# Gated linear attention with a mixture of adapters: a hand-written order of work on all engines, suffix decay, and loads by chunk

## The chip, the cores and the metric

One core of one Trainium2 chip. A core has five engines with an instruction queue each: PE (TensorE, matmuls and transposes), DVE (VectorE), ACT (ScalarE), POOL (GpSimd) and SP (SyncE, which here only issues DMAs). Each runs its queue in order and waits on semaphores for the others. The metric is device time in microseconds of one execution.

## The reference

Four batches, 8 heads, 768 positions, head dimension 48. First a linear attention whose state decays by a gate, then a mixture of 8 adapters of rank 16, of which the best two by a gate count:

```python
for t in range(S):
    state = alpha[:, :, t, :, None] * state + np.einsum('bhd,bhe->bhde', k[:, :, t], v[:, :, t])
    y[:, :, t] = np.einsum('bhd,bhde->bhe', q[:, :, t], state)
...
logits = x @ w_gate                      # x: y with the 8 heads side by side, 3072 x 384
...                                      # softmax over the two largest of 8
delta[mask] += w[mask, k, None] * (x[mask] @ A[e] @ B[e])
return x + delta
```

## The kernel before, in words

A batch has 6 chunks of 128 positions, so there are 24 units (batch, chunk), done in order, since the state passes from chunk to chunk. All 16 input loads (four batches of alpha, k, q, v, 1.18 MB each), the weights and the 24 stores go through SP's queue; batch 3 is issued when the second batch's work begins.

`prologue` (L129) serves two chunks at once. ACT takes the logarithm of alpha (L133); PE sums it along the chunk with a triangular matrix of ones (`cum`, L139) and in total per head pair (L141); ACT makes exp(-cum), exp(cum) and exp(total) (`ainv`, `acum`, `dec`, L145 to L149). POOL multiplies k by `ainv` into `kg` (L151), q by `acum` into `qg` (L153) and casts v into `vb` (L156).

`unit` (L159) does one chunk. PE transposes `kg` and `qg` (`tr`, L165, eight transposes), DVE copies them out (`kq`, L169). PE makes the new state `kv`: an identity matmul brings in the old one (`sbd`, L174), four matmuls add k times v (L179); DVE multiplies by `dec` into the other `sbd` (L186). PE makes the attention scores `at` (L194), DVE masks them (`at_sb`, L198). PE sums `y` from the old state (L206) and from the scores (L214).

Then the mixture: ACT copies `y` out (`xb`, L220), PE transposes it (`xt`, L223), DVE copies that (`xs`, L225), PE makes `z`, the 128 adapter values and 8 gate logits (L228). The gate is a chain on DVE with one stop on ACT: `mx` (L231), `df` (L233), `ex` on ACT (L235), `wu` and its sum `den` (L238), `rd` (L242), `zw` (L244). PE transposes `zw` (`zt`, L248), DVE copies it (`zs`, L250), PE adds the delta into `y` (L251), ACT copies `y` into `o` (L253), SP stores it (L255).

The order of the instructions on each engine is not the order of this text: the framework's scheduler chose it when the program was built, by priority and by its own estimate of when inputs are ready. Once chosen it is fixed. PSUM has one buffer for `cum`, one for `tr`, one for `at` (two banks), two for `y`, and two shared by `kv`, `xt`, `z` and `zt` (tag `m`).

Of the kernel before, what the change touches and what calls it, by code (L numbers as in the profile page):

```python
# [41 lines left out]
def kernel(  # L42
# [86 lines left out]
    def prologue(b, g, ring):  # L129
        a_t, k_t, q_t, v_t = batches[b]  # L130
        cs = slice(g * G, (g + 1) * G)
        lg, qg, kg = lgs[ring], qgs[ring], kgs[ring]
        nc.scalar.activation(lg[:, :, :, 0:D], a_t[:, cs], AF.Ln)  # L133
        acum = scal.tile([P, G, H, D], F4, name="acum")
        ainv = scal.tile([P, G, H, D], F4, name="ainv")
        dec = scal.tile([P, G, NP], F4, name="dec")
        for c in range(G):
            cum = ps_cum.tile([P, 512], F4, name="cum")
            nc.tensor.matmul(cum[:, 0:DM], tri[:, :], lg[:, c, :, 0:D], start=True, stop=True)  # L139
            for p in range(NP):  # L140
                nc.tensor.matmul(  # L141
                    cum[:, DM + p:DM + p + 1],
                    lg[:, c, 2 * p:2 * p + 2, :].rearrange("a b s -> a (b s)"), ones[:, :],
                    start=True, stop=True)
            nc.scalar.activation(  # L145
                ainv[:, c].rearrange("p h d -> p (h d)"), cum[:, 0:DM], AF.Exp, scale=-1.0)
            nc.scalar.activation(  # L147
                acum[:, c].rearrange("p h d -> p (h d)"), cum[:, 0:DM], AF.Exp)
            nc.scalar.activation(dec[:, c, :], cum[:, DM:DM + NP], AF.Exp)  # L149
        for c in range(G):  # L150
            nc.gpsimd.tensor_tensor(  # L151
# [107 lines left out]
    for n, (b, g) in enumerate(duos):  # L259
        if n + 1 < len(duos):  # L260
            nb, ng = duos[n + 1]
            if ng == 0 and nb + 2 < B:
                batches[nb + 2] = load_batch(nb + 2)
# [33 lines left out]
```

## Time and profile before

| | us |
|---|---|
| median of 3 runs | 191.46 (190.2 to 191.65) |
| the profiled execution | 190.65 |
| its span, first to last instruction | 188.9 |
| busy in the span: PE, DVE, ACT, POOL | 109.6, 98.1, 59.0, 59.7 |
| mean granted clock of TensorE (1 is 2.4 GHz) | 0.619 |

Busy time is the time in which an engine has an instruction running. Matmuls are pipelined, so the time of one (0.52 us for 384 columns) is longer than the time for which it keeps the next from starting. In a timeline, "[1.84 <-DVE kq L169]" says that the engine was idle for 1.84 us before, and that DVE's instruction at L169 ended it.

### The profile page before, as it was taken

The numbers are of one execution on the slowest core, as the hardware profiler recorded it, in microseconds if no ns is written. First come the engines' busy times: TensorE is split into PE (matmuls) and PEld (weight loads), VectorE is DVE, ScalarE is ACT, GpSimd is POOL, SyncE is SP. The second block draws the span as 40 slices with busy tenths as digits, with TensorE's granted clock in tenths as the row PEclk, the third lists the DMA queues.
The fourth block names the chain that finished last, engine by engine and source line by source line (L and its number), as shares of the span: only waits on it lengthen the run. The fifth ranks groups of instructions, "written<-read, shape, count | busy, mean of one in ns | idle before, by whom it ended". The sixth has DMA issues, their size and how long they took to land. (4 is left out here: it accounts for less than half of the span.)

```text
span 188.9 us, 2870 instructions
## 1 busy us (share of the span) xinstructions
PE 109.6 (58%) x1064; PEld 77.1 (41%) x1064; DVE 98.1 (52%) x284; ACT 59.0 (31%) x157; POOL 59.7 (32%) x77
## 2 busy tenths in 40 slices
PE   0133677585646665675468855774776675565631
PEld 0021464354424434543346534444544453454410
DVE  0001677656435476644084776646646647465550
ACT  2472020732650311420721622432334312221221
POOL 6048830320486120450612810351255320400000
PEclk9999999967555555555555555555557655555555
DMA  4999988989989889990021011101101110110111
GB/s 122 263 265 266 167 242 230 253 252 257 257 235 268 255 237 260 260 300 3 0 83 42 3 42 42 43 0 45 42 0 42 45 42 0 45 45 13 54 58 42
DMA packets 31966, 24.18 MB, mean 128 GB/s; under 512 B 4176, under 2 KB 31952, under 8 KB 31952
## 3 DMA queue, kind: packets, MB, share of 16 engines
q1 hardware_dynamic: 31952, 24.00, 43.8%
q8 instruction: 8, 0.13, 0.3%
q14 instruction: 6, 0.05, 0.1%
HBM read 19.28 MB, written 4.72 MB: 127 GB/s over the span
## 5 line engine op out<-in xcount | busy, mean ns | idle before, releaser
L151 POOL TENSOR_TENSOR kg<-k_t,ainv 128x384 bf16<-128x384 f32 x24 | 23.8, 998 | 75.0 <-ACT ainv L145 38.2
L169 DVE COPY kq<-tr 128x1024 bf16<-128x1024 bf16 x24 | 16.5, 687 | 34.2 <-PE tr L165 27.2
L198 DVE TENSOR_TENSOR at_sb<-at,mask 128x1024 bf16<-128x1024 f32 x24 | 29.4, 1224 | 5.0 <-PE at L194 3.0
L194 PE MATMUL at<-kq 48*128 48x128 bf16 x192 | 15.7, 299 | 22.4 <-DVE kq L169 17.8
L253 ACT COPY o<-y 128x384 f32<-128x384 f32 x24 | 11.4, 481 | 55.3 <-PE y L251 36.0
L153 POOL TENSOR_TENSOR qg<-q_t,acum 128x384 bf16<-128x384 f32 x24 | 23.6, 998 | 3.4 <-ACT acum L147 2.8
L139 PE MATMUL cum<-lg,tri 128*128 128x384 bf16 x24 | 11.4, 476 | 18.4 <-ACT dec L149 10.0
L165 PE MATMUL tr<-ident,kg 128*128 128x128 bf16 x96 | 15.0, 296 | 11.0 <-POOL kg L151 10.2
L220 ACT CAST xb<-y 128x384 bf16<-128x384 f32 x24 | 11.5, 482 | 28.6 <-PE y L214 28.6
L194 PEld LDWEIGHTS <-kq 48*128 48x128 bf16 x192 | 8.6, 123 | 28.8 <-DVE kq L169 22.5
L165 PE MATMUL tr<-ident,qg 128*128 128x128 bf16 x96 | 16.2, 303 | 3.8 <-POOL qg L153 3.8
L186 DVE TENSOR_TENSOR sbd<-kv,dec 64x192 bf16<-64x192 f32 x40 | 14.2, 355 | 7.7 <-PE kv L179 5.8
L156 POOL CAST vb<-v_t 128x768 bf16<-128x768 f32 x12 | 9.8, 823 | 25.6 <-PE kv L179 11.3
L231 DVE MAX8 mx<-z 128x8 f32<-128x8 f32 x24 | 4.2, 175 | 22.1 <-PE z L228 22.0
L145 ACT ACTIVATE ainv<-cum 128x384 f32<-128x384 f32 x24 | 11.8, 492 | 11.7 <-PE cum L141 10.7
L141 PEld LDWEIGHTS <-lg 128*128 128x128 bf16 x96 | 7.4, 118 | 18.3 <-issue 18.1
L248 PE MATMUL zt<-ident,zw 128*128 128x128 bf16 x24 | 6.9, 286 | 13.7 <-DVE zw L244 13.1
L214 PE MATMUL y<-vb,at_sb 128*128 128x48 bf16 x192 | 14.3, 217 | 0.5 <-ACT o L253 0.5
L165 PEld LDWEIGHTS <-kg 128*128 128x128 bf16 x96 | 8.0, 125 | 15.1 <-POOL kg L151 12.7
L206 PE MATMUL y<-sbd,kq 128*128 128x96 bf16 x80 | 10.9, 271 | 4.9 <-ACT o L253 4.8
L147 ACT ACTIVATE acum<-cum 128x384 f32<-128x384 f32 x24 | 11.7, 488 | 4.0 <-POOL qg L153 4.0
L228 PE MATMUL z<-W,xs 128*128 128x136 bf16 x72 | 12.7, 314 | 0.5 <-DVE xs L225 0.5
(43 smaller groups left out, 180.1 us busy)
## 6 DMA issues: line engine op xcount, KB each, us to landing
out_dram<-o SPq DMA_DIRECT2D x24, 192.0 KB, 1.9
W_st<-in_moe_A_dram SPq DMA_DIRECT2D x3, 64.0 KB, 2.9
B_st<-in_moe_B_dram SPq DMA_DIRECT2D x1, 192.0 KB, 2.6
a_t<-in_alpha_dram SPq DMA_DIRECT2D x4, 0.2 KB, 7.1
k_t<-in_k_dram SPq DMA_DIRECT2D x4, 0.2 KB, 10.2
q_t<-in_q_dram SPq DMA_DIRECT2D x4, 0.2 KB, 10.2
v_t<-in_v_dram SPq DMA_DIRECT2D x4, 0.2 KB, 9.9
W_st<-in_moe_w_gate_dram SPq DMA_DIRECT2D x1, 12.0 KB, 2.4
```

Of the source, the lines that this page charges most:

```text
L145: nc.scalar.activation(ainv[:, c].rearrange("p h d -> p (h d)"), cum[:, 0:DM], AF.Exp, scale=-1.0)
L147: nc.scalar.activation(acum[:, c].rearrange("p h d -> p (h d)"), cum[:, 0:DM], AF.Exp)
L151: nc.gpsimd.tensor_tensor(out=kg[:, c, :, 0:D], in0=k_t[:, g * G + c], in1=ainv[:, c], op=ALU.mult)
L153: nc.gpsimd.tensor_tensor(out=qg[:, c, :, 0:D], in0=q_t[:, g * G + c], in1=acum[:, c], op=ALU.mult)
L165: nc.tensor.transpose(tr[:, w, p, :], src[:, ci, 2 * p:2 * p + 2, :].rearrange("a b s -> a (b s)"), ident[:, :])
L169: nc.vector.tensor_copy(out=kq, in_=tr)
L186: nc.vector.tensor_tensor(out=sbd[(c + 1) % 2][rows, :, hh, :], in0=kv[rows, :, hh, :], in1=_bc(dec[rows, ci, :], D), op=ALU.mult)
L194: nc.tensor.matmul(at[:, hh, p, :], kq[rows, 0, p, :], kq[rows, 1, p, :], start=True, stop=True)
L198: nc.vector.tensor_tensor(out=at_sb.rearrange("p a b t -> p (a b) t"), in0=at.rearrange("p a b t -> p (a b) t"), in1=_bc_mid(mask[:, :], ( ...
L214: nc.tensor.matmul(y[:, h * D:(h + 1) * D], at_sb[:, hh, p, :], vb[:, ci, h, :], start=first, stop=False, skip_group_check=True)
L220: nc.scalar.copy(xb, y)
L228: nc.tensor.matmul(z, xs[:, i, :], W[:, i, :], start=(i == 0), stop=(i == NF - 1))
```

## The change

- The scheduler is switched off (`tc.manual_schedule()`). The work of a unit is cut into 32 pieces, and the table `STEP` says in which order a step of the new loop issues them, and for which unit: step n with (z, -1) issues `z` of unit n-1, with (kgm, 2) the product `kg` of unit n+2. The order holds for each engine's queue.
- Decay by suffix: `cum` is summed with a strictly lower triangle (`suf`), so it is what decays after a position to the end of the chunk. `kg` is k times exp(cum), `qg` is q times exp(-cum). The state is decayed ahead of its use, by POOL (`sdm`: `sdec` = `sbd` times `dec`), and DVE adds `kv` to it (`state`); the identity matmul is gone.
- The pieces work on one chunk, not on two, save the logarithm of the later batches. `kg` and `qg` have three buffers.
- ACT copies `z` from PSUM to SBUF (`zc`), and the gate reads that copy. `xs` and `zs` move from DVE to ACT.
- PSUM: one tag `m` with 4 buffers for `z`, `tr`, `cum`, `zt`, `xt`, `kv`. `o` has 5 buffers.
- Loads: batch 0 comes in 24 loads, chunk by chunk (alpha, k, q, v). Eight of them stand ahead of the weights, the rest behind them, then alpha, k and q of batch 1; each step from n = 0 on issues one more of the remaining nine, behind its store.

The core of the diff; the functions left out hold the lines of before, one function for each.

```diff
-    outp = ctx.enter_context(tc.tile_pool(name="outp", bufs=3))
+    outp = ctx.enter_context(tc.tile_pool(name="outp", bufs=5))
     PS = bass.MemoryType.PSUM
-    ps_cum = ctx.enter_context(tc.tile_pool(name="ps_cum", bufs=1, space=PS))
-    ps_tr = ctx.enter_context(tc.tile_pool(name="ps_tr", bufs=1, space=PS))
+    ps_s = ctx.enter_context(tc.tile_pool(name="ps_s", bufs=1, space=PS))
...
+    def load(b, i, c=None, eng=None):
+        name, src = SRC[i]
+        if raw[b][i] is None:
+            raw[b][i] = loads.tile([P, H * NCH, 64], F4, name=name, tag=name)
+            batches[b][i] = raw[b][i].rearrange("p (h c) d -> p c h d", h=H)[:, :, :, 0:D]
+        if c is None:
+            (eng or nc.sync).dma_start(
+                out=raw[b][i][:, :, 0:D], in_=src[b].rearrange("h (c j) d -> j (h c) d", j=C))
+        else:
+            (eng or nc.sync).dma_start(
+                out=batches[b][i][:, c],
+                in_=src[b][:, c * C:(c + 1) * C, :].rearrange("h j d -> j h d"))
+
+    def by_chunk(b):
+        order = [(0, 0)]
+        for c in range(NCH):
+            order += [(1, c), (2, c), (0, c + 1), (3, c)]
+        return [(b, i, c) for i, c in order if c < NCH]
+
+    def by_tensor(b):
+        return [(b, i) for i in range(4)]
+
+    queue = by_chunk(0) + by_tensor(1) + by_tensor(2) + by_tensor(3)
+    for x in queue[:8]:
+        load(*x, eng=nc.sync)
...
-    batches[1] = load_batch(1)
-    batches[2] = load_batch(2)
-
-    tri = consts.tile([P, P], F2, name="tri")
-    nc.gpsimd.memset(tri, 1.0)
+    for x in queue[8:27]:
+        load(*x)
+    queue = queue[27:]
+
+    suf = consts.tile([P, P], F2, name="suf")
+    nc.gpsimd.memset(suf, 1.0)
     nc.gpsimd.affine_select(
-        out=tri, in_=tri, compare_op=ALU.is_ge, fill=0.0, base=0,
-        pattern=[[1, P]], channel_multiplier=-1,
+        out=suf, in_=suf, compare_op=ALU.is_gt, fill=0.0, base=0,
+        pattern=[[-1, P]], channel_multiplier=1,
...
+    def ln(u):
+        b, c = units[u]
+        if b in (0,):
+            nc.scalar.activation(
+                lgs[(u // G) % 2][:, u % G, :, 0:D], batches[b][0][:, c], AF.Ln)
+        elif u % G == 0:
+            nc.scalar.activation(
+                lgs[(u // G) % 2][:, :, :, 0:D], batches[b][0][:, c:c + G], AF.Ln)
+
+    def cum(u):
+        s = st[u]
+        lg = lgs[(u // G) % 2][:, u % G]
+        cum = ps_s.tile([P, 512], F4, name="cum", tag="m", bufs=4)
+        nc.tensor.matmul(cum[:, 0:DM], suf[:, :], lg[:, :, 0:D], start=True, stop=True)
+        for p in range(NP):
+            nc.tensor.matmul(
+                cum[:, DM + p:DM + p + 1],
+                lg[:, 2 * p:2 * p + 2, :].rearrange("a b s -> a (b s)"), ones[:, :],
+                start=True, stop=True)
+        s["cum"] = cum
...
+    def edec(u):
+        s = st[u]
+        s["dec"] = scal.tile([P, NP], F4, name="dec", bufs=6)
...
+    def kgm(u):
+        s = st[u]
+        b, c = units[u]
+        s["kg"] = kgs[u % RING]
+        nc.gpsimd.tensor_tensor(
+            out=s["kg"][:, :, 0:D], in0=batches[b][1][:, c], in1=s["up"], op=ALU.mult)
...
+    def sdm(u):
+        s = st[u]
+        b, c = units[u]
+        if c > 0:
+            nc.gpsimd.tensor_tensor(
+                out=sdec[c % 2].rearrange("p a b d -> p a (b d)"),
+                in0=sbd[c % 2].rearrange("p a b d -> p a (b d)"),
+                in1=_bc(s["dec"][:, :], 2 * D), op=ALU.mult)
...
+    def kv(u):
+        s = st[u]
+        b, c = units[u]
+        if c + 1 == NCH:
+            return
+        s["kv"] = ps_s.tile([P, NP, 2, D], F4, name="kv", tag="m", bufs=4)
+        for p in range(NP):
+            nc.tensor.matmul(
+                s["kv"][:, p].rearrange("p b d -> p (b d)"), pair(s["kg"], p), pair(s["vb"], p),
+                start=True, stop=True)
...
+    def state(u):
+        s = st[u]
+        b, c = units[u]
+        if c + 1 == NCH:
+            return
+        for hh in range(2):
+            rows = slice(HP * hh, HP * hh + HP)
+            dst, src = sbd[(c + 1) % 2][rows, :, hh, :], s["kv"][rows, :, hh, :]
+            if c == 0:
+                nc.vector.tensor_copy(out=dst, in_=src)
+            else:
                 nc.vector.tensor_tensor(
-                    out=sbd[(c + 1) % 2][rows, :, hh, :], in0=kv[rows, :, hh, :],
-                    in1=_bc(dec[rows, ci, :], D), op=ALU.mult)
-
-        at = ps_at.tile([P, 2, NP, P], F4, name="at")
+                    out=dst, in0=src, in1=sdec[c % 2][rows, :, hh, :], op=ALU.add)
...
+                    sdec[c % 2][:, p].rearrange("p b d -> p (b d)"),
...
+    def xs(u):
+        s = st[u]
+        s["xs"] = moep.tile([P, NF, P], F2, name="xs")
+        nc.scalar.copy(s["xs"], s["xt"])
...
+    def zc(u):
+        s = st[u]
+        s["zc"] = moep.tile([P, NW], F4, name="zc")
+        nc.scalar.copy(s["zc"], s["z"])
+
+    def gmx(u):
+        s = st[u]
+        s["mx"] = moep.tile([P, 8], F4, name="mx")
+        nc.vector.max(s["mx"], s["zc"][:, E * R:NW])
...
+            out=s["wu"], in0=s["zc"][:, E * R:NW], scalar=s["mx"][:, 1:2], in1=s["ex"],
+            op0=ALU.is_ge, op1=ALU.mult, accum_out=s["den"])
...
+            out=s["zw"], in0=s["zc"][:, 0:E * R].rearrange("p (e r) -> p e r", e=E),
+            scalar=s["rd"][:, 0:1], in1=_bc(s["wu"][:, :], R), op0=ALU.mult, op1=ALU.mult)
...
+    STEP = (
+        (z, -1), (zc, -1), (gmx, -1), (sdm, 0), (gdf, -1), (gex, -1), (kgm, 2), (tr, 1),
+        (kq, 1), (cum, 3), (gwu, -1), (grd, -1), (ln, 5), (edn, 3), (gzw, -1), (qs, 0), (av, 0),
+        (at, 1), (zt, -1), (xb, 0), (zs, -1), (edec, 3), (xt, 0), (kv, 0), (xs, 0), (qgm, 3),
+        (msk, 1), (eup, 3), (delta, -1), (fin, -1), (state, 0), (vbc, 3),
+    )
+    with tc.manual_schedule():
+        for n in range(-6, NU + 3):
+            for f, off in STEP:
+                u = n + off
+                if 0 <= u < NU:
+                    f(u)
+            for _ in range(1 if n >= 0 else 0):
+                if queue:
+                    load(*queue.pop(0))
```

## Rows read from the trace of the kernel before

**Rows 1.** Page, part 1: busy us, share of span, instructions.
```profile
PE 109.6 (58%) x1064; PEld 77.1 (41%) x1064; DVE 98.1 (52%) x284; ACT 59.0 (31%) x157; POOL 59.7 (32%) x77
```

**Rows 2.** Instructions of line L253, durations ns min/median/max, first and last start us.
```profile
L253 ACT COPY o<-y x24: 479/480/509, 33.2 to 185.5; 128x384 f32<-128x384 f32 x24
```

**Rows 3.** Waits: who for whom, us in total, times, longest us.
```profile
ACT o L253 <- PE y L251: 36.0, 15, 3.9
```

**Rows 4.** Timeline of a steady stretch: start us, us, engine, line, operation.
```profile
114.88 0.52 PE L228 MATMUL z<-W,xs 128*128 128x136 bf16 x3
...
115.43 0.17 DVE L231 MAX8 mx<-z 128x8 f32<-128x8 f32 x1 [1.54 <-PE z L228]
...
115.71 1.23 DVE L198 TENSOR_TENSOR at_sb<-at,mask 128x1024 bf16<-128x1024 f32 x1
...
116.85 0.22 DVE L233 TENSOR_SCALAR df<-z,mx 128x8 f32<-128x8 f32 x1
116.99 0.68 DVE L169 COPY kq<-tr 128x1024 bf16<-128x1024 bf16 x1
117.17 0.21 ACT L235 ACTIVATE ex<-df 128x8 f32<-128x8 f32 x1 [0.92 <-DVE df L233]
117.58 0.22 DVE L238 SCALAR_TENSOR_TENSOR wu<-z,mx,ex 128x8 f32<-128x8 f32 x1
...
118.45 0.29 PE L248 MATMUL zt<-ident,zw 128*128 128x128 bf16 x1
...
118.53 0.52 PE L174 MATMUL kv<-sbd,ident 128*128 128x384 bf16 x1
...
119.49 0.52 PE L223 MATMUL xt<-ident,xb 128*128 128x128 bf16 x3
...
120.17 0.36 DVE L225 COPY xs<-xt 128x384 bf16<-128x384 bf16 x1
...
120.50 0.52 PE L139 MATMUL cum<-lg,tri 128*128 128x384 bf16 x1
...
120.82 0.54 PE L228 MATMUL z<-W,xs 128*128 128x136 bf16 x3
```

**Rows 5.** Groups by line and form: busy us, mean ns, idle before.
```profile
L220 ACT CAST xb<-y 128x384 bf16<-128x384 f32 x24 | 11.5, 482 | 28.6 <-PE y L214 28.6
...
L156 POOL CAST vb<-v_t 128x768 bf16<-128x768 f32 x12 | 9.8, 823 | 25.6 <-PE kv L179 11.3 <-PE y L214 8.7 <-issue 5.7
```

**Rows 6.** Instructions that read tile k_t: ns min/median/max, first and last start.
```profile
L151 POOL TENSOR_TENSOR kg<-k_t,ainv x24: 994/998/1005, 12.2 to 162.3; 128x384 bf16<-128x384 f32 x24
```

**Rows 7.** Timeline of SP's queue while it issues batch 1.
```profile
22.29 0.71 SPq L77 DMA_DIRECT2D a_t<-in_alpha_dram  x1
...
28.80 4.40 SPq L77 DMA_DIRECT2D q_t<-in_q_dram  x1
33.65 4.23 SPq L77 DMA_DIRECT2D v_t<-in_v_dram  x1
```

**Rows 8.** Page, part 6: DMA issues, KB each, median us to landing.
```profile
a_t<-in_alpha_dram SPq DMA_DIRECT2D x4, 0.2 KB, 7.1
...
v_t<-in_v_dram SPq DMA_DIRECT2D x4, 0.2 KB, 9.9
```

**Rows 9.** Timeline of the last unit.
```profile
182.14 0.52 PE L228 MATMUL z<-W,xs 128*128 128x136 bf16 x3
...
185.54 0.48 ACT L253 COPY o<-y 128x384 f32<-128x384 f32 x1 [2.10 <-PE y L251]
```

**Rows 10.** Windows: busy us of PE, PEld, DVE, ACT, POOL; clock, DMA share, GB/s.
```profile
22.00:24.00 2.00, 1.17 (x12) 0.77 (x8) 1.75 (x2) 0.00 (x0) 0.89 (x2) 1.00 0.79 129
...
100.00:110.00 10.00, 7.84 (x77) 5.75 (x76) 5.99 (x17) 4.42 (x12) 4.78 (x5) 0.50 0.07 26
...
140.00:150.00 10.00, 7.32 (x83) 5.45 (x80) 5.94 (x18) 3.77 (x11) 5.06 (x6) 0.67 0.06 21
```

**Rows 11.** Timeline of a stretch with a higher clock.
```profile
37.08 0.33 PE L139 MATMUL cum<-lg,tri 128*128 128x384 bf16 x1
```

More of the change, by code (lines that the diff above doesn't have):

```diff
@@ L27 @@
 G = 2
+RING = 3
+NU = B * NCH
 def _bc(src: bass.AP, rep: int) -> bass.AP:
@@ L127 @@
     nc.vector.tensor_copy(out=B_all, in_=B_st)
[L129 to L139, printed above, removed]
-            for p in range(NP):
[L141 to L151, printed above, removed]
-                out=kg[:, c, :, 0:D], in0=k_t[:, g * G + c], in1=ainv[:, c], op=ALU.mult)
-            nc.gpsimd.tensor_tensor(
-                out=qg[:, c, :, 0:D], in0=q_t[:, g * G + c], in1=acum[:, c], op=ALU.mult)
-        vb = vpool.tile([P, G, H, D], F2, name="vb")
-        nc.gpsimd.tensor_copy(out=vb, in_=v_t[:, cs])
-        return qg, kg, vb, dec
@@ L214, in unit @@
                 nc.tensor.matmul(
-                    y[:, h * D:(h + 1) * D], at_sb[:, hh, p, :], vb[:, ci, h, :],
-                    start=first, stop=False, skip_group_check=True)
-                first = False
-        xb = moep.tile([P, DM], F2, name="xb")
-        nc.scalar.copy(xb, y)
-        xt = ps_m.tile([P, NF, P], F2, name="xt", tag="m")
-        for i in range(NF):
-            nc.tensor.transpose(xt[:, i, :], xb[:, i * P:(i + 1) * P], ident[:, :])
-        xs = moep.tile([P, NF, P], F2, name="xs")
@@ L247, in unit @@
-        zt = ps_m.tile([P, P], F2, name="zt", tag="m")
-        nc.tensor.transpose(zt, zw.rearrange("p e r -> p (e r)"), ident[:, :])
-        zs = moep.tile([P, P], F2, name="zs")
-        nc.vector.tensor_copy(out=zs, in_=zt)
-        nc.tensor.matmul(y, zs[:, :], B_all[:, :], start=False, stop=True, skip_group_check=True)
+                    s["y"][:, h * D:(h + 1) * D], s["at_sb"][:, hh, p, :], s["vb"][:, h, :],
+                    start=(c == 0 and h == 0), stop=False, skip_group_check=True)
@@ new lines, in xb, with xt, z @@
+    def xb(u):
+        s = st[u]
+        s["xb"] = moep.tile([P, DM], F2, name="xb")
+        nc.scalar.copy(s["xb"], s["y"])
+    def xt(u):
+        s = st[u]
+        s["xt"] = ps_s.tile([P, NF, P], F2, name="xt", tag="m", bufs=4)
+        for i in range(NF):
+            nc.tensor.transpose(s["xt"][:, i, :], s["xb"][:, i * P:(i + 1) * P], ident[:, :])
+    def xs(u):
+        s = st[u]
+        s["xs"] = moep.tile([P, NF, P], F2, name="xs")
+        nc.scalar.copy(s["xs"], s["xt"])
+    def z(u):
+        s = st[u]
+        s["z"] = ps_s.tile([P, NW], F4, name="z", tag="m", bufs=4)
+        for i in range(NF):
+            nc.tensor.matmul(
+                s["z"], s["xs"][:, i, :], W[:, i, :], start=(i == 0), stop=(i == NF - 1))
@@ new lines, in zt, with zs, delta, fin @@
+    def zt(u):
+        s = st[u]
+        s["zt"] = ps_s.tile([P, P], F2, name="zt", tag="m", bufs=4)
+        nc.tensor.transpose(s["zt"], s["zw"].rearrange("p e r -> p (e r)"), ident[:, :])
+    def zs(u):
+        s = st[u]
+        s["zs"] = moep.tile([P, P], F2, name="zs")
+        nc.scalar.copy(s["zs"], s["zt"])
+    def delta(u):
+        s = st[u]
+        nc.tensor.matmul(
+            s["y"], s["zs"][:, :], B_all[:, :], start=False, stop=True, skip_group_check=True)
+    def fin(u):
+        s = st[u]
+        b, c = units[u]
@@ L252, in unit @@
         o = outp.tile([P, DM], F4, name="o")
-        nc.scalar.copy(o, y)
+        nc.scalar.copy(o, s["y"])
         t0 = b * S + c * C
         nc.sync.dma_start(out=out[t0:t0 + C, :], in_=o)
-    duos = [(b, g) for b in range(B) for g in range(NCH // G)]
-    pros = {0: prologue(0, 0, 0)}
[L259 to L263, printed above, removed]
-            pros[n + 1] = prologue(nb, ng, (n + 1) % 2)
-        for c in range(g * G, (g + 1) * G):
-            unit(b, c, pros[n])
+        s.clear()
```

161 lines of the change are left out of this document (91 added, 70 removed).

## The prediction

> **What bounds the kernel now.** I read the page's busy shares first [rows 1]. Per unit (24 of them) they give PE 109.6 / 24 = 4.57 us, DVE 98.1 / 24 = 4.09, ACT 2.46, POOL 2.49. The pace is another: the last instruction of a unit, ACT's copy `o`, first starts at 33.2 us and last at 185.5 [rows 2], so (185.5 - 33.2) / 23 = 6.62 us a unit. No engine fills that, so a chain sets it. The waits name its end [rows 3]: ACT's `o` waited 36.0 us in 15 cases for PE's last matmul of the unit (L251).
>
> The timeline of one steady stretch shows the chain [rows 4]. Follow the gate of the mixture from one `z` to the next: 114.88 to 120.82, 5.94 us. Four pieces of it are not the gate's own work:
> - `mx` ends at 115.60 (115.43 + 0.17); `df`, which needs only `mx`, starts at 116.85. The 1.23 us mask product `at_sb` stands between them on DVE: about 1.2 us lost.
> - `ex` ends at 117.38 (117.17 + 0.21); `wu` starts at 117.58, because `kq` (116.99) is in front of it on DVE: about 0.2 us lost.
> - `zt` starts at 118.45 and holds PE for 0.08; `xt`, whose input was long ready, starts at 119.49. The identity matmul that brings the old state into `kv` (118.53), the `kv` matmuls and the delta matmul have their place in between: 0.95 us lost.
> - `xs` ends at 120.53 (120.17 + 0.36); `z` starts at 120.82, behind `cum` (120.50): about 0.25 us lost.
>
> So the present order puts about 2.6 us of other work into each turn of the gate's chain.
>
> **The change, part by part.** Step n is one pass of the new loop. It runs `z` to `fin` for unit n-1; `sdm`, `qs`, `av`, `xb`, `xt`, `kv`, `xs`, `state` for unit n; `tr`, `kq`, `at`, `msk` for unit n+1; `cum` and its exponentials for unit n+3.
>
> *Order.* In a step PE does z, tr, cum, qs, av, at, zt, xt, kv, delta; DVE gmx, gdf, kq, gwu, grd, gzw, msk, state; ACT zc, gex, ln, edn, xb, zs, edec, xs, eup, fin. I lay the chain out from the start of `z`, with the durations of rows 4:
> - `z` is read 0.55 after its start (114.88 to 115.43, of which 0.03 is the hop from engine to engine). The reader is now ACT's copy `zc`, which before doesn't have. Its price lies between ACT's 8 columns (`ex`, 0.21) and 384 (`xb`, 0.48 [rows 5]); on that line 136 columns give 0.30. `gmx` starts at 0.55 + 0.30 + 0.03 = 0.88.
> - `gmx` 0.17, `gdf` 0.22 and `gex` 0.21 with a hop each: `gex` ends at 1.54.
> - `kq` is DVE's next. `cum`'s 384 columns hold PE 0.32 (120.50 to 120.82), 0.83 ns a column. So `tr`, behind `z`'s 408 columns, starts at 0.34, streams 1,024 columns and is readable at 0.34 + 0.85 + 0.2 = 1.4 (0.2 is what `xt`'s 0.52 has over its 384 columns). `kq` runs to 2.1.
> - `gwu` starts there, `zt` 0.87 later (117.58 to 118.45), at 2.97; `xt` follows directly, 3.05, and is read 0.55 later, 3.60.
> - `xs`, now on ACT at the price of `xb`: ends at 4.08.
> - `eup` follows on ACT, again 384 columns: 4.56. The next `z` waits for it: the shared PSUM tag has 4 slots and a step takes six, so `z` takes the slot of the `cum` four tiles earlier, whose last reader is `eup`. A step is 4.6.
>
> The other path, `av` to `xb` to `xt`, gives no more: 2,588 columns in front of `xb` are 2.15 us, with 0.2 to drain and 0.48 for `xb` it would let `xt` start at 2.9. A second way, from the losses: 5.94 - 2.6, plus `zc` 0.33, `xs` on ACT 0.12 longer, `eup` 0.48, and about 0.5 where `gwu` now waits for `kq`: 4.77. I take 4.7, between the two.
>
> *Engines.* They stay under it. DVE loses `xs`, 0.36, and `zs`: below 3.7. ACT gains `xs` 0.48, `zs` and `zc` some 0.30 each: 2.46 + 1.08 = 3.5. PE has about 4,900 columns, at most 4.1 us. POOL gains the pre-decay `sdm`, which the trace of before doesn't show: at most a product of as many elements, 1.0 [rows 6], at least a cast, 0.82 / 2 = 0.41 [rows 5]. I take 1.0, the row of the same operation: 2.49 + 20/24 = 3.3. It is hidden: it starts when `state` is done, 0.3 into the step, and `qs` needs it at about 1.65. With that slack of 0.3 gone, the excess would go straight into the step.
>
> *Suffix decay.* It removes the identity matmul (counted above) and swaps which exponential multiplies k and which q. Otherwise the same instructions in the same sizes: nothing.
>
> *Loads.* The same bytes are ahead of batch 1's v in SP's queue as before: batch 0, the weights, batch 1's a, k, q. Before it is issued at 33.65 us [rows 7] and lands 9.9 later [rows 8], at 43.5. Batch 0 by chunk lets the first steps start sooner, but step 1 has `ln` of unit 6 in ACT's fixed order, which needs batch 1's a: 22.29 + 7.1 = 29.4 [rows 7, 8]. Steps 2 and 3 follow at the pace. POOL's step 3 ends with `vbc`, which needs that v at 43.5; behind it in POOL's queue is `sdm` of step 4. So `qs` of step 4 comes at 43.5 + 0.41 + 1.0 = 45.0, and with 4.7 - 1.65 left of that step, step 5 starts at 48. Nothing waits for loads after that: batch 2's a is needed in step 7 (57 us), its v in step 9 (67), while a load takes 4.85 (28.80 to 33.65) and one is released in each step behind a store: 43.5 + 4 x 4.85 = 63.
>
> *Sum.* Steps 5 to 23 are 19 x 4.7 = 89.3. Step 24 is the bare gate chain, now 182.14 to 185.54 and 0.48 [rows 9], 3.88; `zc` makes it 4.2. From the end of the last `o` (186.02) to the end of the span, 188.9, are 2.9. So 48 + 89.3 + 4.2 + 2.9 = 144.4 of span. The profiled execution took 190.65 for its span of 188.9, 1.75 more: **146 us**. That execution lies 0.4% under the median of 191.46.
>
> **The rivals.**
> - *A faster PE clock.* The granted clock is 0.50, that is 1.2 GHz, at 100:110, and between the two levels at 140:150 [rows 10]. In a fast stretch 384 columns last 0.33 us [rows 11] against 0.52 (120.50). The layout then loses 0.15 at `z`, 0.3 in front of `kq` and 0.1 at `xt`: 4.1 a step, 48 + 19 x 4.1 + 7.1 + 1.75 = 135 us. For it: PE works more densely. Against it: the dense 7.84 of 10 us at 100:110 stayed at 0.50.
> - *DVE and POOL hold each other up.* `gwu` and `gzw` now read two tensors from SBUF (`zc` with `ex`, `zc` with `wu`), and `gdf` goes from SBUF to SBUF; until now `z` was in PSUM. If such an instruction had to wait for POOL's running product, `gdf` would wait until `sdm` ends at 1.3, and `gzw`, due at 2.6, for `qgm`, which runs from 2.7, when `edn` and POOL's `kgm` are done and `gwu` is over, to 3.7. `zt` would come at 4.1 instead of 2.97 and the step at 5.7: 48 + 19 x 5.7 + 7.1 + 1.75 = 165 us. No row of before has such a pair, so nothing speaks against it. The Trainium skill has it as a rule (SBUF — State Buffer, section SBUF: two separate sides): GpSimd and a VectorE instruction with two SBUF inputs, or in a mode that uses both ports, take one port pair as an exclusive lock, and the loser waits for the whole instruction. By the rule it would be 165 us, by the bare rows 146; no run so far shows which.
> - *Loads by chunk are slower.* The weights' short rows came at 129 GB/s with a DMA share of 0.79 [rows 10]. If the 24 chunks went like that, their 4.7 MB would take 36 us instead of 18, and all that waits for batch 1 would come up to 18 later: at most 164 us. Against it: a chunk has the same rows of 192 bytes as a whole load.
> - *Slower than before.* With 48 + 7.1 + 1.75 fixed, the step would have to exceed (190.65 - 56.85) / 19 = 7.04 us. That happens if DVE and POOL exclude each other in every instruction: 3.7 + 3.3 and hops, near 7.2, make 194 us. It decides from about 2.4 us of mutual waiting in each step on. Against it: POOL's 24 products took 994 to 1005 ns each [rows 6], though DVE worked beside many of them.
>
> **How the numbers follow.** The forecast (139 to 153) gets 0.47, the port rival (153 to 171) 0.31, slow chunks (150 to 164) 0.10, the fast clock (134 to 139) 0.07, full exclusion 0.03, anything else 0.02. The range 134 to 168 takes in all but the last two and a little of the second, nearly 0.9: its low end is the fast clock, its high end the port rival with a step of 5.85. Faster by over 1% (about what a measurement of this kernel can tell from no change) 0.94, within 1% 0.02, slower 0.04.
>
> **What would show it.** In the changed kernel's profile: `z` starts 4.7 us apart after 50 us; `xt` directly behind `zt`; POOL waits for batch 1's v until about 43.5, and no wait for a load comes later. `zc` near 0.30 and `sdm` near 1.0. The port rival would show `gwu` far over `wu`'s 0.22, `gzw` with it, or POOL's products over 1.0; the clock rival a granted clock over 0.9 after 50 us; the chunk rival batch 1's a landing after 35 us. The forecast is wrong if `z` waits for anything but `eup` or `xs`, or if DVE has no gaps left.

## The result, and the profile after

| | before | after |
|---|---|---|
| median of the runs compared | 190.83 us | 146.01 us (145.55 to 147.08) |
| ratio, with 95% interval | | 0.767 [0.760, 0.774] |
| the profiled execution, its span | 190.65, 188.9 us | 146.4, 144.7 us |
| mean granted clock of TensorE | 0.619 | 0.795 |

Times here and below are medians of all runs of a kernel; a ratio leaves out runs that took over 1.5% longer than the fastest of the same kernel, so it need not be the quotient of two medians.

The forecast was 146 us. Its sum came out; two of its terms did not, and their errors nearly cancelled. So the profile after is read term by term.

The busy times from the page's first part, and the DMA line of its second (compare [rows 1] for the first):

```profile
PE 87.1 (60%) x1048; PEld 64.4 (45%) x1048; DVE 96.4 (67%) x236; ACT 77.3 (53%) x232; POOL 77.7 (54%) x111
DMA packets 50718, 24.18 MB, mean 167 GB/s; under 512 B 29072, under 2 KB 50704, under 8 KB 50704
```

DVE is busy for almost as long as before, though `xs` and `zs` have gone to ACT, and now for longer than any other engine. In the steady part it has few gaps: 76.03 of the 90 us from 50 to 140 are busy. These are two stretches of the view by windows (stretch, its length, busy time with count of PE, weight loads, DVE, ACT and POOL; granted clock, DMA share, GB/s):

```profile
60.00:70.00 10.00, 7.73 (x99) 5.68 (x96) 9.17 (x22) 7.11 (x23) 6.70 (x9) 0.74 0.80 217
100.00:110.00 10.00, 7.69 (x95) 5.61 (x95) 9.17 (x21) 6.70 (x23) 7.36 (x10) 0.79 0.12 42
```

The timeline of two turns of the gate, from `z` to `z`, of the kernel after (start, duration, engine, line, operation; [rows 4] are one turn of before). Lines of other work are left out:

```profile
96.32 0.48 ACT L321 COPY xs<-xt 128x384 bf16<-128x384 bf16 x1
96.70 0.50 ACT L184 ACTIVATE up<-cum 128x384 f32<-128x384 f32 x1
96.86 0.52 PE L327 MATMUL z<-W,xs 128*128 128x136 bf16 x3
97.44 0.30 ACT L333 COPY zc<-z 128x136 f32<-128x136 f32 x1
97.58 0.82 POOL L221 TENSOR_TENSOR sdec<-sbd,dec 128x384 bf16<-128x384 bf16 x1 [0.34 <-DVE sbd L264]
97.78 0.17 DVE L338 MAX8 mx<-zc 128x8 f32<-128x8 f32 x1 [0.34 <-ACT zc L333]
97.98 0.45 DVE L343 TENSOR_SCALAR df<-zc,mx 128x8 f32<-128x8 f32 x1
98.37 1.00 POOL L201 TENSOR_TENSOR kg<-k_t,up 128x384 bf16<-128x384 f32 x1
98.47 0.69 DVE L240 COPY kq<-tr 128x1024 bf16<-128x1024 bf16 x1
98.47 0.21 ACT L348 ACTIVATE ex<-df 128x8 f32<-128x8 f32 x1 [0.73 <-DVE df L343]
98.50 0.48 PE L292 MATMUL y<-sdec,kq 128*128 128x96 bf16 x4
99.07 0.32 DVE L354 SCALAR_TENSOR_TENSOR wu<-zc,mx,ex 128x8 f32<-128x8 f32 x1
99.64 0.35 DVE L366 SCALAR_TENSOR_TENSOR zw<-zc,rd,wu 128x128 bf16<-128x128 f32 x1
100.04 0.23 PE L373 MATMUL zt<-ident,zw 128*128 128x128 bf16 x1 [0.43 <-DVE zw L366]
100.21 0.34 PE L316 MATMUL xt<-ident,xb 128*128 128x128 bf16 x3
100.59 0.48 ACT L321 COPY xs<-xt 128x384 bf16<-128x384 bf16 x1
100.96 0.50 ACT L184 ACTIVATE up<-cum 128x384 f32<-128x384 f32 x1
101.12 0.35 PE L327 MATMUL z<-W,xs 128*128 128x136 bf16 x3 [0.16 <-ACT xs L321]
103.64 0.99 POOL L208 TENSOR_TENSOR qg<-q_t,dn 128x384 bf16<-128x384 f32 x1
103.95 0.84 DVE L366 SCALAR_TENSOR_TENSOR zw<-zc,rd,wu 128x128 bf16<-128x128 f32 x1
```

What the reader is to see here:

- Three of the four pieces of other work that stood inside the gate's chain are gone from it: `df` follows `mx` at once, `xt` follows `zt`, `z` follows `xs`. The fourth, `kq`, still stands in front of `wu` (`ex` ends at 98.68, `wu` starts at 99.07). The next `z` after these starts at 105.88, so the two turns take 4.26 and 4.76 us (101.12 - 96.86, 105.88 - 101.12), where before one took 5.94.
- `z` waits for `xs` and nothing else: at 96.86 and 101.12 it starts 0.05 us after `xs` ends (96.80, 101.07), while `up` is still running. So it is in all 24 units, save that in the last three there is no `up` to run beside it.
- `df` on 8 columns takes 0.45 us, twice as long as before, and ends at 98.43, where POOL's `sdec` ends (98.40). `wu` ends at 99.39, where POOL's `kg` ends (99.37). In the first turn `zw` meets no product of POOL at its start and takes 0.35; in the second `qg` has started before it, and `zw` takes 0.84, to 104.79, with `qg` ending at 104.63.
- Over all 24 units it is the same. 50 of the 72 `df`, `wu` and `zw` start while an instruction of POOL runs; every one of them ends just behind that instruction, `df` and `wu` by 0.02 to 0.03 us, `zw` by 0.15. The other 22 take 0.21 to 0.23 us (`df`, `wu`) and 0.35 (`zw`), also where a product of POOL starts in the middle of them.

The start and the end of the steady stretch, from the timeline (the first line is `z` of step 5, the second that of step 24, the third the last copy of the program):

```profile
51.92 0.52 PE L327 MATMUL z<-W,xs 128*128 128x136 bf16 x3
137.55 0.52 PE L327 MATMUL z<-W,xs 128*128 128x136 bf16 x3 [0.17 <-ACT xs L321]
141.36 0.48 ACT L389 COPY o<-y 128x384 f32<-128x384 f32 x1 [0.59 <-PE y L382]
```

Nineteen steps lie between the first two: (137.55 - 51.92) / 19 = 4.51 us each. The last unit takes 141.84 - 137.55 = 4.29, and 144.7 - 141.84 = 2.86 follow. With 51.92 these make the span of 144.7.

The start is late because of loads. Two waits from the timeline, batch 1's alpha and v:

```profile
34.38 0.84 ACT L166 ACTIVATE lg<-a_t 128x768 bf16<-128x768 f32 x1 [4.93 <-DMA a_t<-in_alpha_dram]
48.49 0.50 POOL L215 CAST vb<-v_t 128x384 bf16<-128x384 f32 x1 [2.55 <-DMA v_t<-in_v_dram]
```

And the groups by form (busy us, mean ns of one | idle before):

```profile
L366 DVE SCALAR_TENSOR_TENSOR zw<-zc,rd,wu 128x128 bf16<-128x128 f32 x24 | 13.8, 576 | 0.8
L343 DVE TENSOR_SCALAR df<-zc,mx 128x8 f32<-128x8 f32 x24 | 10.7, 446 | 0.8
L354 DVE SCALAR_TENSOR_TENSOR wu<-zc,mx,ex 128x8 f32<-128x8 f32 x24 | 6.9, 288 | 0.7 <-ACT ex L348 0.7
L333 ACT COPY zc<-z 128x136 f32<-128x136 f32 x24 | 7.4, 307 | 0.6 <-PE z L327 0.5
L221 POOL TENSOR_TENSOR sdec<-sbd,dec 128x384 bf16<-128x384 bf16 x20 | 16.6, 828 | 15.0 <-DVE sbd L264 12.9 <-DVE sbd L262 2.2
```

Before, with `z` in PSUM, the first three took 351, 222 and 221 ns. They are 0.225 + 0.224 + 0.067 = 0.52 us longer per unit now, 12.4 us in 24 units. So DVE's busy time is as long as before although its work is less.

### The profile page after: what moved, and what is told of

It is laid out like the page before. It is cut to its first block, busy times and chain, and to the rows that moved or that the text cites. A ratio compares the mean times of both kernels' runs of the same rounds, so it can differ in the third digit from the quotient of the medians.

```text
span 144.7 us, 2946 instructions
## 1 busy us (share of the span) xinstructions
PE 87.1 (60%) x1048; PEld 64.4 (45%) x1048; DVE 96.4 (67%) x236; ACT 77.3 (53%) x232; POOL 77.7 (54%) x111
## 2 busy tenths in 40 slices
DMA packets 50718, 24.18 MB, mean 167 GB/s; under 512 B 29072, under 2 KB 50704, under 8 KB 50704
## 4 chain that ended last, share of the span: by engine, by line
DVE 31%; SPq 25%; ACT 20%; PE 7%; DMA 7%; issue 7%; POOL 1%; ACTq 0%; POOLq 0%
SPq L91 14%; DVE kq L240 8%; DVE zw L366 8%; SPq L88 8%; DMA v_t<-in_v_dram 7%; DVE df L343 6%; ACT up L184 5%; ACT o L389 5%; PE zt L373 4%; ACT xs L321 3%; DVE wu L354 3%; ACT zc L333 3%; ACT zs L378 3%; DVE mx L338 2%; DVE rd L361 2%
## 5 line engine op out<-in xcount | busy, mean ns | idle before, releaser
L208 POOL TENSOR_TENSOR qg<-q_t,dn 128x384 bf16<-128x384 f32 x24 | 24.0, 999 | 27.6 <-ACT dn L189 18.0
L221 POOL TENSOR_TENSOR sdec<-sbd,dec 128x384 bf16<-128x384 bf16 x20 | 16.6, 828 | 15.0 <-DVE sbd L264 12.9
L201 POOL TENSOR_TENSOR kg<-k_t,up 128x384 bf16<-128x384 f32 x24 | 24.0, 1000 | 0.8 <-ACT up L184 0.8
L234 PE MATMUL tr<-ident,kg 128*128 128x128 bf16 x96 | 12.9, 277 | 10.9 <-POOL kg L201 10.9
L215 POOL CAST vb<-v_t 128x384 bf16<-128x384 f32 x24 | 12.1, 504 | 13.1 <-PE kv L249 8.7
L173 PE MATMUL cum<-lg,suf 128*128 128x384 bf16 x24 | 10.9, 455 | 6.7 <-ACT lg L163 6.7
L264 DVE TENSOR_TENSOR sbd<-kv,sdec 64x192 bf16<-64x192 f32 x32 | 11.2, 352 | 5.2 <-PE kv L249 4.9
L316 PE MATMUL xt<-ident,xb 128*128 128x128 bf16 x72 | 9.7, 255 | 8.2 <-ACT xb L310 8.1
L378 ACT COPY zs<-zt 128x128 bf16<-128x128 bf16 x24 | 6.4, 266 | 15.4 <-PE zt L373 15.2
L373 PE MATMUL zt<-ident,zw 128*128 128x128 bf16 x24 | 6.0, 249 | 14.1 <-DVE zw L366 13.9
L366 DVE SCALAR_TENSOR_TENSOR zw<-zc,rd,wu 128x128 bf16<-128x128 f32 x24 | 13.8, 576 | 0.8
L348 ACT ACTIVATE ex<-df 128x8 f32<-128x8 f32 x24 | 5.0, 208 | 17.4 <-DVE df L343 17.4
L292 PE MATMUL y<-sdec,kq 128*128 128x96 bf16 x80 | 8.6, 247 | 8.1 <-POOL sdec L221 8.1
```

Of the source, the lines that this page charges most:

```text
L201: nc.gpsimd.tensor_tensor(out=s["kg"][:, :, 0:D], in0=batches[b][1][:, c], in1=s["up"], op=ALU.mult)
L208: nc.gpsimd.tensor_tensor(out=s["qg"][:, :, 0:D], in0=batches[b][2][:, c], in1=s["dn"], op=ALU.mult)
L215: nc.gpsimd.tensor_copy(out=s["vb"], in_=batches[b][3][:, c])
L221: nc.gpsimd.tensor_tensor(out=sdec[c % 2].rearrange("p a b d -> p a (b d)"), in0=sbd[c % 2].rearrange("p a b d -> p a (b d)"), in1=_bc(s[" ...
L234: nc.tensor.transpose(t[:, w, p, :], pair(src, p), ident[:, :])
L366: nc.vector.scalar_tensor_tensor(out=s["zw"], in0=s["zc"][:, 0:E * R].rearrange("p (e r) -> p e r", e=E), scalar=s["rd"][:, 0:1], in1=_bc( ...
```

## The experiments

Each changes the kernel after, save the two that change the kernel before. The kernel before took 189.65 to 190.84 us beside them.

**Is the time in the gate's reads from SBUF?** The gate's copy `zc` goes to a free part of `z`'s PSUM bank. The copy and the order stay; only what the gate reads is no longer in SBUF.

```diff
-        s["z"] = ps_s.tile([P, NW], F4, name="z", tag="m", bufs=4)
+        s["zz"] = ps_s.tile([P, 512], F4, name="z", tag="m", bufs=4)
+        s["z"] = s["zz"][:, 0:NW]
...
-        s["zc"] = moep.tile([P, NW], F4, name="zc")
+        s["zc"] = s["zz"][:, 256:256 + NW]
```

> The changed kernel, with ACT's copy zc written into the unused half of z's own PSUM bank instead of SBUF; ACT's work and the order are the same, but the gate's instructions on DVE now have one SBUF tensor at most. If they are long (df 446 ns, wu 288, zw 576 in the mean, against 222, 221 and 351 before) because DVE and POOL exclude each other, all three go back to 0.22, 0.22 and 0.35 us; 0.51 us leave the chain of each unit, and with 0.3 to 0.5 of them on the path the time is 136 to 140 us. If they are long for another reason, or off the path, 145 to 147 us.

Measured: 139.03 us (136.06 to 140.3; too far apart for an interval). The groups by form of this kernel:

```profile
L367 DVE SCALAR_TENSOR_TENSOR zw<-z,rd,wu 128x128 bf16<-128x128 f32 x24 | 8.4, 350 | 0.8
L344 DVE TENSOR_SCALAR df<-z,mx 128x8 f32<-128x8 f32 x24 | 5.4, 226 | 0.8
L355 DVE SCALAR_TENSOR_TENSOR wu<-z,mx,ex 128x8 f32<-128x8 f32 x24 | 5.2, 218 | 0.6 <-ACT ex L349 0.6
```

All three have their durations of before again, also where they start while POOL runs, and the step falls from 4.51 to 4.22 ((131.66 - 51.48) / 19, by the starts of `z`). So the longer durations come from operands in SBUF beside running instructions of POOL. They cost 7 us by the medians. The size is uncertain: the fastest of the four runs took 136.06 us, and the profiled one, at 140.3, was the slowest. In it three of the 19 turns take 5.4 to 5.9 us, because ACT's `o` waits for a buffer whose store is not done (4.6 us in 3 cases, none in after); the middle one of the 19 takes 4.04, against 4.40 in after.

**And without the copy at all?** The gate reads `z` in PSUM, as before the change.

```diff
-        s["zc"] = moep.tile([P, NW], F4, name="zc")
-        nc.scalar.copy(s["zc"], s["z"])
+        s["zc"] = s["z"]
```

> The changed kernel without zc: the gate reads z in PSUM, as before the change. If zc's only price is its own time in the chain (0.30 us a unit), 146 - 19 x 0.3 = 140 us; if the mutual exclusion of DVE and POOL, which zc in PSUM took away for 7 us, goes as well, the two add: 146 - 7 - 6 = 133 us. With the clock low in more of the time, since PE does the same in less, 135 to 137.

Measured: 136.81 us, ratio 0.713 [0.705, 0.721]. The step is 3.94 ((125.93 - 51.01) / 19). The copy was meant to cost 0.30 on the chain. By the medians its going gives 2.2 us, but the ranges of the two kernels overlap (134.41 to 138.5 here), and the run profiled here is the fastest of its four, that of the kernel before it the slowest. So the difference of 0.28 between the two steps is not a measure of it, and that the copy's whole 0.30 comes back is not shown. What is late next, from the waits (total us, times, longest):

```profile
PE y L292 <- POOL sdec L221: 14.3, 15, 4.0
```

In after that wait was 8.1 us in 9 cases: now that the gate is shorter, the attention's first matmuls wait longer for the pre-decay on POOL.

**Does a faster TensorE clock shorten the step?** A further matmul per step, in front of `zt`, keeps PE busy where it waits for DVE. It writes into the free part of `z`'s PSUM bank (`zz`, as in the first run), and its result is not used.

```diff
...
+        nc.tensor.matmul(
+            s["zz"][:, NW:512], ident[:, :], B_all[:, 0:512 - NW], start=True, stop=True)
```

> The changed kernel with one more matmul of 376 columns a unit, into the unused part of z's bank and ahead of zt, where PE waits for zw; its result is not used. If PE's clock (0.795 in the mean) is held down by these waits and PE's part of the chain sets the pace, the clock rises to 0.9 or more and the time falls to 139 to 143 us. If DVE and its waits set the pace, the clock rises and the time stays at 145 to 147. If the filler itself is in the way, 148 or more.

Measured: 145.48 us, ratio 0.766 [0.760, 0.771], against 0.767 for after. The mean granted clock rose from 0.795 to 0.881 and the time stayed. The added matmul is seldom in the way: in 18 of 24 units PE still waits for `zw` behind it (8.4 us in all, 13.9 in after). So PE does not pace a step at this order; DVE, busy for 9.07 us in 100:110 here too, and what it waits for do. In the two kernels with the gate in PSUM the clock was higher as well (0.843 and 0.924 in the profiled runs); what it gave there is not separated.

**What are the two copies on ACT worth?** `xs` and `zs` go back to DVE, at their places in the order.

```diff
-        nc.scalar.copy(s["xs"], s["xt"])
+        nc.vector.tensor_copy(out=s["xs"], in_=s["xt"])
...
-        nc.scalar.copy(s["zs"], s["zt"])
+        nc.vector.tensor_copy(out=s["zs"], in_=s["zt"])
```

> The changed kernel with xs and zs copied by DVE, as before, in the same places of the order. DVE's work grows by 0.58 us a unit, from 96 to 110 us. If DVE paces a step (it is 80 to 90% busy after 50 us), 19 x 0.5 = 10 us are added: 155 us. If the chain through z, zw and xt paces it and DVE has room, the copies are shorter there (0.36 and 0.22 instead of 0.48 and 0.27) and the time is 143 to 147.

Measured: 162.12 us, ratio 0.856 [0.850, 0.862]: 16 us, more than forecast. DVE is busy for 114.2 us, and those who wait for it wait longer (from the waits; in after the first two lines were 17.4 and 12.9, the third 8.1):

```profile
ACT ex L348 <- DVE df L343: 39.6, 24, 2.1
...
POOL sdec L221 <- DVE sbd L264: 24.7, 14, 4.5
PE y L292 <- POOL sdec L221: 23.8, 20, 2.2
```

`xs` in 8.6 us and `zs` in 5.4 are 14.0 us of DVE's time, and `df` grew from 446 to 639 ns, another 4.6: together 18.6, near to the 17.8 by which DVE's busy time and to the 16 by which the kernel's grew. DVE has new waits too, for `zt` in front of `zs` (8.9 us) and for `xt` in front of `xs` (8.6), but its idle time in all did not grow (160.2 - 114.2 = 46.0 us, 144.7 - 96.4 = 48.3 in after). So on an engine with so few gaps, work that is added shows nearly in full.

The same move alone in the kernel before:

```diff
-        nc.vector.tensor_copy(out=xs, in_=xt)
+        nc.scalar.copy(xs, xt)
...
-        nc.vector.tensor_copy(out=zs, in_=zt)
+        nc.scalar.copy(zs, zt)
```

> The kernel before, with xs and zs copied by ACT instead of DVE and nothing else changed. With the scheduler's order the changed kernel takes 162 us, 28 less than before; this asks how much of the 28 is this move. If DVE's place in the gate's chain is what it frees (0.58 us of 6.6 a unit, at 24 units 14 us), 176 to 182 us. If the chain stays behind at_sb and kq all the same, 187 to 191.

Measured: 188.69 us, ratio 0.985 [0.979, 0.992]. DVE's busy time fell from 98.1 to 84.2 us, and the kernel gained 2. Where a chain of waits sets the pace, the same 14 us are nearly free.

**What does the hand-written order do?** The scheduler is left on; pieces, buffers, engines and loads are those of after.

```diff
-    with tc.manual_schedule():
+    if True:
```

> The changed kernel with the scheduler switched on again: the same 32 pieces, buffers and loads, but the framework's own order on every engine. If the hand-written order carries the gain, other work stands in the gate's chain again: 6 us or more from one z to the next and 170 to 190 us. If the rest of the change (no identity matmul, four shared PSUM buffers, three buffers for kg and qg, work by one chunk) carries it, 145 to 155 us.

Measured: 161.87 us, ratio 0.852 [0.847, 0.857], between the two forecasts. So some 28 of the 45 us come without the fixed order, and 16 with it. DVE has 99.0 us of work here, but the step is longer, (153.33 - 19.01) / 23 = 5.84 us over all units, and the time lies in waits between the engines:

```profile
POOL vb L215 <- PE kv L249: 25.7, 11, 4.0
PEld L373 <- DVE zw L366: 20.7, 22, 2.3
```

The two numbers hide two larger ones. The scheduler's order starts its first `z` at 19.01, the fixed one at 27.76 (before: 28.11). From step 5 to step 24 the fixed order takes 85.6 us, the scheduler's 111.4 (41.89 to 153.33). So the fixed order wins 26 us in the steps and gives 10 back at the start, and 9 of the scheduler's 28 us against before are its earlier start. Its turns are not slow throughout either: the last eight take 4.0 to 5.3 us, the eight ahead of them 6.1 to 7.6. Why those, stays open.

**What gives the 28 us?** Not the copies alone, as shown. One other part was tried in the kernel before: `cum` and `tr` in the shared PSUM tag with 4 buffers.

```diff
-    ps_cum = ctx.enter_context(tc.tile_pool(name="ps_cum", bufs=1, space=PS))
-    ps_tr = ctx.enter_context(tc.tile_pool(name="ps_tr", bufs=1, space=PS))
...
-    ps_m = ctx.enter_context(tc.tile_pool(name="ps_m", bufs=2, space=PS))
+    ps_m = ctx.enter_context(tc.tile_pool(name="ps_m", bufs=4, space=PS))
```

> The kernel before, with cum, tr, kv, xt, z and zt in one PSUM tag of four buffers as in the changed kernel, instead of one, one and two. If the second buffer that tr and cum get lets the scheduler run PE ahead of DVE, most of the 28 us that the scheduler's order keeps in the changed kernel come from it: 168 to 178 us. If PSUM was not what held units apart, 187 to 191, or more where z gets its buffer late.

Measured: 235.05 us, ratio 1.230 [1.225, 1.236], far beyond both forecasts. In 24 of 24 units PE, DVE and ACT now wait for each other in turn:

```profile
ACT xb L218 <- PE y L212: 64.4, 24, 9.5
...
DVE kq L167 <- PE tr L163: 47.7, 24, 17.3
...
PE zt L246 <- DVE zw L242: 40.1, 24, 1.7
```

With one tag for all, the scheduler's order became nearly serial. So the shared tag alone is no gain. Which of the remaining parts, the work by single chunks, three buffers of `kg` and `qg`, or the missing identity matmul, brings the 28 us, or whether they do it only together with the copies, stays open; the 9 us of earlier start, which batch 0 by chunk would explain, were not tried alone.

**Does the suffix decay cost something?** The triangle and the exponentials are those of before again, the identity matmul brings the old state into `kv`, DVE multiplies by `dec`, and POOL's `sdm` is gone. Order and loads stay.

```diff
-        if c > 0:
+        if False:                            # sdm
...
+        if c > 0:
+            nc.tensor.matmul(
+                s["kv"].rearrange("p a b d -> p (a b d)"), ident[:, :],
+                sbd[c % 2].rearrange("p a b d -> p (a b d)"),
+                start=True, stop=False, skip_group_check=True)
...
-                    out=dst, in0=src, in1=sdec[c % 2][rows, :, hh, :], op=ALU.add)
+            nc.vector.tensor_tensor(
+                out=dst, in0=src, in1=_bc(s["dec"][rows, :], D), op=ALU.mult)
```

> The changed kernel with the decay as before: a triangle for the sum from the chunk's start, the identity matmul that brings the state into kv, DVE's product with dec, and no pre-decay on POOL. If the identity matmul on PE is what the suffix decay saves, it costs 0.16 to 0.32 us a unit now: 149 to 152 us. If it hides behind the chain in the new order, since kv stands behind xt, 145 to 147. If POOL's pre-decay costs more than it saves, by holding up df, 140 to 144.

Measured: 141.85 us, ratio 0.744 [0.736, 0.752]: the decay by suffix costs about 4 us. The step is 4.22 ((132.98 - 52.87) / 19). POOL is busy for 62.4 us instead of 77.7, and DVE is held up less, although it still reads `zc` in SBUF (`zw` keeps its 567 ns):

```profile
L346 DVE TENSOR_SCALAR df<-zc,mx 128x8 f32<-128x8 f32 x24 | 8.1, 339 | 0.8
L357 DVE SCALAR_TENSOR_TENSOR wu<-zc,mx,ex 128x8 f32<-128x8 f32 x24 | 5.2, 217 | 0.7 <-ACT ex L351 0.7
```

`df` and `wu` are 107 and 71 ns shorter than in after, 4.3 us in 24 units, which is about what the kernel gained. So it is work on POOL that lengthens them, here that of `sdm`.

**Do the loads by chunk delay the start?** Batch 0 in four loads ahead of the weights, as before; the rest as after.

```diff
-    queue = by_chunk(0) + by_tensor(1) + by_tensor(2) + by_tensor(3)
-    for x in queue[:8]:
+    queue = by_tensor(0) + by_tensor(1) + by_tensor(2) + by_tensor(3)
+    for x in queue[:4]:
...
```

> The changed kernel with batch 0 loaded by four whole tensors as before. If the loads by chunk cost the 5 us by which batch 1 landed later than forecast (a at 34.4 instead of 29.4, v at 48.5 instead of 43.5), v lands at 43.5 to 44, step 5 starts at 48 instead of 51.9 and the time is 142 us. If the early start that the chunks give is worth more, since whole k, q and v of batch 0 land at 12, 16.5 and 21 us, 148 us or more.

Measured: 144.19 us, ratio 0.759 [0.754, 0.764]. The packets and the wait for batch 1's v of this kernel:

```profile
DMA packets 31966, 24.18 MB, mean 169 GB/s; under 512 B 4176, under 2 KB 31952, under 8 KB 31952
44.81 0.50 POOL L215 CAST vb<-v_t 128x384 bf16<-128x384 f32 x1 [0.58 <-DMA v_t<-in_v_dram]
```

That v is there 3.7 us sooner (44.81 for 48.49), and step 5 starts at 49.26 instead of 51.92, though the very first unit starts later (`z` at 30.71, not 27.76). The number of packets is that of before; by chunk there are 18,752 more. So the loads by chunk gain nothing here. What they cost is 1 to 2 us and not clear of the noise: the intervals touch (after: [0.760, 0.774]), and the next run, with the same packets as after, took 144.9.

The trace of after shows why the early chunks give so little. Unit 0's `y` is complete at 22.93 us, but ACT's fixed order has the logarithm of the unit five ahead in front of its copy `xb`, and that waits for the alpha of the last chunk:

```profile
25.37 0.52 ACT L163 ACTIVATE lg<-a_t 128x384 bf16<-128x384 f32 x1 [2.21 <-DMA a_t<-in_alpha_dram]
...
26.17 0.47 ACT L310 CAST xb<-y 128x384 bf16<-128x384 f32 x1
```

In the same way unit 1 stands behind batch 1's alpha (34.38). With the scheduler's order, which is not bound to this, the same loads gave the first `z` at 19.01. This is read from the traces; a fixed order with a shorter reach was not run.

Their rows go to places six chunks apart in SBUF, so this was tried next: the chunk's 8 heads side by side.

```diff
-            batches[b][i] = raw[b][i].rearrange("p (h c) d -> p c h d", h=H)[:, :, :, 0:D]
+            batches[b][i] = raw[b][i].rearrange(
+                "p (c h) d -> p c h d" if b == 0 else "p (h c) d -> p c h d", h=H)[:, :, :, 0:D]
```

> The changed kernel with batch 0's tiles laid out chunk by chunk in SBUF, so that the eight rows of a chunk lie 256 bytes apart as in a whole load, not 1,536. If the packets of 192 bytes come from that distance, packets under 512 bytes fall from 29,072 to about 4,500, batch 1's a lands at 29 to 30 us and the time is 142. If they come from the form of the load itself (8 rows for a partition instead of 48), the packets stay at 29,000 and the time at 146.

Measured: 144.9 us, ratio 0.765 [0.762, 0.768], and the same 50,718 packets, 29,072 of them short. The distance of the rows is not the cause. A load with 8 rows to a partition is cut into more packets than one with 48; why, stays open.

**Do the gains add up?** Gate from PSUM without the copy, and decay by prefix:

> The changed kernel without zc and with the decay as before. Each alone gave 146.0 to 136.8 and 146.0 to 141.9 us. If the prefix form gains because POOL's pre-decay holds up df through the shared access to SBUF, the gate in PSUM has taken that gain already: 136 to 138 us. If it gains because qs waits for the pre-decay (14.3 us of waits of PE for it with the gate in PSUM), the two add: 131 to 134.

Measured: 134.28 us, ratio 0.703 [0.699, 0.706]. The prefix gave 4.2 us alone; on top of the gate from PSUM it gives 2.5 by the medians, and the intervals touch ([0.705, 0.721] there), so how much is left is open. What it saved alone was for the most part the waiting of DVE for POOL, which is gone already. And the shorter turns (the middle one of 19 takes 3.60 us, 3.83 with the gate from PSUM alone) run into the stores: `o` waits for a buffer for 9.3 us in 5 cases, there for 4.9 in 3.

With whole loads besides:

> The same with batch 0 loaded by four whole tensors. Alone that gave 146.0 to 144.2 us. If the end is paced by steps that start when batch 1's v has landed, 2 us less than the run without it. If the shorter steps now run into the loads of batches 2 and 3, which are released one per step, the gain goes: within 1 us of it.

Measured: **131.34 us**, ratio 0.687 [0.684, 0.691], the fastest of all, 10% under the kernel after. A turn of its gate, from the timeline:

```profile
96.88 0.35 PE L330 MATMUL z<-W,xs 128*128 128x136 bf16 x3
97.58 0.17 DVE L340 MAX8 mx<-z 128x8 f32<-128x8 f32 x1
97.79 0.23 DVE L345 TENSOR_SCALAR df<-z,mx 128x8 f32<-128x8 f32 x1
...
98.99 0.35 DVE L368 SCALAR_TENSOR_TENSOR zw<-z,rd,wu 128x128 bf16<-128x128 f32 x1
...
100.70 0.35 PE L330 MATMUL z<-W,xs 128*128 128x136 bf16 x3 [0.38 <-ACT xs L324]
```

A turn takes 3.82 here. Its next limit is in the waits:

```profile
ACT o L391 <- DMA out_dram<-o: 8.9, 5, 3.5
```

The copy `o` waits for a buffer whose store is not done. Stores and loads share SP's queue, and with loads under way SP takes 4.3 to 5.5 us to issue one store (71.95 to 76.91 for one of them in this timeline). Three of the 19 turns take 5.0 to 7.2 us for such waits and for a late v.

## Why the prediction was right, and where it was not

The sum: predicted 48 + 89.3 + 4.2 + 2.9 = 144.4, measured 51.9 + 85.6 + 4.3 + 2.9 = 144.7. The start was 3.9 us too early in the forecast, the 19 steps 3.7 us too long. The result was right to 0.3 us; the two large terms were each off by over ten times that. That it came out so close is luck.

- **What bounds the kernel.** Right in the main: of the four pieces of other work in the gate's chain ([rows 4]) three left it where the order was fixed, and the turns became shorter. But the order alone is 16 of the 45 us; what the other 28 took away was not traced to the chain.
- **The step, 4.7.** Measured 4.51. The layout up to `xs` was nearly exact: predicted 0.55 to the copy, 2.97 to `zt`, 3.05 to `xt`, 4.08 to the end of `xs`; the turn at 96.86 has 0.58, 3.18, 3.35 and 4.21. That is the shorter kind of turn; where `zw` meets `qg`, as in the next, all from `zt` on comes 0.5 later. The step that failed is the next: "The next `z` waits for it", for `eup`, because of the PSUM slot. It never does. `z` runs at 96.86 and 101.12 while `up` (from 96.70 and 100.96) still runs. So the slot that `z` takes is not the one which `eup` still reads; which one it is, stays open. Without that term the layout gives 4.1, and the measured turns are 4.26 and 4.76.
- **The port rival.** True, in a smaller size. It was put at 5.7 - 4.7 = 1.0 us a step, with `gzw` behind the whole of `qgm` each time. It holds, but `zw` meets a product in some turns and not in others (0.35, then 0.84), and `df` is held by part of `sdm`. Reading from PSUM saves 0.29 a step in the mean and 7 us by the medians. The Trainium skill (SBUF — State Buffer, section SBUF: two separate sides) calls the port pair of VectorE and GpSimd an exclusive lock, held for the whole instruction. The trace agrees: those of `df` and `wu` that start while POOL runs all end within 0.03 us of the end of POOL's instruction. That POOL was ever held up in turn, no row shows: its `kg` and `qg` took 0.99 to 1.01 us. So the false wait for `eup` and the port's real one stood in for each other: 0.48 too much and some 0.3 to 0.4 too little. The prediction had named "DVE has no gaps left" as a sign of its being wrong; at 9.17 of 10 us that came close to true.
- **The clock rival.** Half true: the granted clock rose from 0.619 to 0.795. It was priced at 0.6 us a step; the run with the further matmul shows that at this order more of it (0.881) gives nothing that can be measured. Nor did it in the kernel before: of its runs beside the last experiments one had 0.795 and took 190.44 us, two had 0.63 and took 190.79 and 190.84.
- **DVE "below 3.7" of 4.7.** Right for its own work: with the gate in PSUM it is busy for 83.0 us, 3.46 a unit. In this kernel it is 96.4 us, 4.02 a unit, with the waits for POOL inside its instructions, and in 100:110 they fill 9.17 of 10 us. That few gaps are left fits the run in which the clock rose and the step did not shorten.
- **`sdm` 1.0 and hidden; suffix decay nothing.** `sdm` took 0.83, between the bounds. The slack of 0.3 that was named does not hold: in the turn at 96.86 `sdm` ends after 1.54 us instead of 1.3, and `qs` starts right behind it, after 1.64. Its price was put at nothing and is some 4 us: without it and with prefix decay the kernel is 4.2 us faster. By 4.3 us `df` and `wu` become shorter there: `sdm` holds up `df`, and so pushes `wu` behind the start of `kg`. Whether it also costs time through `qs` is not shown.
- **`zc` 0.30, `zs` 0.30, `xs` 0.48.** Measured 0.31, 0.27, 0.48. `vb` by one chunk 0.50 for 0.41.
- **Loads, step 5 at 48.** Measured 51.92. "The same bytes are ahead of batch 1's v" was right and not enough: alpha landed at 34.38 (29.4 predicted), v at 48.49 (43.5). SP issued that alpha at 26.50, not at 22.29, and that v at 38.22, not at 33.65 ([rows 7]). From that v to step 5 it took 3.4 us instead of 4.5, so this term has a small cancelling of its own. That is the rival of slow chunks, at 4 to 5 us instead of 18. Against it had been said that a chunk has the same rows of 192 bytes; the packets show that it does not move them alike.
- **Slower than before.** It had 0.03, and nothing came near it: POOL's products kept their 1.00 us, and the mutual waiting was 0.5 us a unit where 2.4 were needed.
